# A third PSUM bank for one of five chains of products, and the work list of a fused convolution and SiLU layer written anew

## The chip, the cores and the metric

The kernel runs on one core of one Trainium2 chip. The metric is the device time of one launch in microseconds, as the median of several runs. All arithmetic is in fp32.

## The reference, cut to what matters

A causal depthwise convolution over time (seven taps, softmaxed per head), followed by a two-layer feed-forward block with SiLU:

```python
x: (8, 4096, 192)   weight: (8 heads, 7 taps)   w_in: (192, 2048)   w_out: (2048, 192)
w = softmax(weight, axis=-1)
conv[b, s, h, :] = sum_k w[h, k] * x_pad[b, s + k, h, :]      # six zeros ahead of each sequence
x1 = conv.reshape(32768, 192)
h  = x1 @ w_in                    # 32768 x 192 x 2048
g  = h / (1 + exp(-h))
out = g @ w_out                   # 32768 x 2048 x 192
```

## The kernel before, in words

**Tiling.** The 32768 tokens are cut into 32 blocks of 1024, and each block into two halves of 512. The 192 input channels are three pieces of 64, so a product of `h` contracts 64 rows: it uses half of TensorE's rows, and two products, one on partitions 0 to 63 ("row A") and one on 64 to 127 ("row B"), run side by side. The 2048 hidden channels are sixteen chunks of 128. Fifteen of these are worked in five groups of three, and one, the "plain" chunk, by itself.

**The products of h.** For a group, three chunks times two token halves are six outputs. Done directly they would need 18 products; the kernel does 15, from sums of weights (made once) and sums of inputs (`wins`, made for each block by VectorE). Token `P r.g` of the work list is product `r` of group `g` (line 623 in the profile). Eight or nine of the fifteen (`ON_B`) stand on row B. Products are added up in PSUM in three chains for a group, written in `CHAINS`: chain 0 is products 5, 2, 6, 1, 0, 14, in this order and all on row B (one exception: 14 of group 4); chain 1 is 3, 9, 7, 4, 8, all but 4 on row A; chain 2 is 12, 10 on row A. Products 13 and 11 go on top of sums that VectorE wrote to banks 5 and 6.

A chain's partial sums are read between its products. After product 5, 2, 6, 1 and 0 of chain 0 ScalarE copies the bank to a tile `u` (tokens `u5` to `u0`, line 672), after 14 it takes the SiLU (`S3`). Chains 1 and 2 are read by VectorE (tokens `X`, `a`, `b`, line 666), which adds or subtracts them to those `u`. So the next product of a chain, which writes to the same bank, waits for the engine that reads it. `S` tokens are the other SiLUs (line 684). The plain chunk is nine matmuls `L` (line 640), three of full width and three pairs of halves, in banks 7 and 3, evicted by the SiLUs `SL`.

**The output.** `g @ w_out` is done in tokens `D i.je` (line 739): each is four matmuls on four column groups of 32, which run side by side, over all 128 rows. There are 48 of them for a block, of one 512-wide slot each, except the eight with `i` = 5, which are 128 wide. Some read sums `t` that VectorE makes (line 707); the results are merged (`M`, `x`, `y`, `z`), turned (`o`) and stored (`st`). Output tile `osb` and the sums `t` share one pool of three buffers, in rotation.

An fp32 matmul stands in the trace as two passes, each with its weight load.

**The order.** Nothing is scheduled by the program: the order is a list, kept on every engine. `START` is the list for the first blocks, `PLAN` is run once for each later block, and each token issues its instructions in turn. A sign says whose work it is: none, the block itself; `-` one block back, `=` two back, `+` the next one. `ld` loads inputs, `i` turns them, `ha` sets the halo, `v` is one tap of the convolution, `sp` copies the result to both row groups (`dup`), `w` makes the input sums; all five are for the block after the one that their sign names. TensorE thus does, for each run of `PLAN`, one long row of 64-row products and one row of output products. In the list of before the output products are broken once: after twelve of them stand `-P8.3` and `P2.0`, then come the other 36.

**The banks.** PSUM has eight banks of 512 fp32 columns, all used. `chain_bank` gives chain `c` of group `g` its bank: the groups are taken in the order `QUEUE = (0, 4, 1, 2, 3)`, and

```python
    def chain_bank(g, c):
        return banks[(c * 2 + QUEUE.index(g) % 2) if c < 2 else 4]
    PLAIN_BANKS = (7, 7, 3)
    ACC = (7, 1, 3, 5, 6, 4, 0)      # banks of the output sums
```

so chain 0 has banks 0, 1, 0, 1, 0 for the five groups, chain 1 has 2, 3, 2, 3, 2, and chain 2 has 4.

Of the kernel before, what the change touches and what calls it, by code (L numbers as in the profile page):

```python
# [17 lines left out]
def kernel(  # L18
# [60 lines left out]


    PLAN = (
        "P5.0 v.20 -t.01 | -P10.3 -S3.2 | -P4.3 -S1.1 -S0.1 -sp.2 -a0.2 | -D1.31 u5.0 -t.03 "
        "-S4.3 | -D2.01 -S2.3 -t.02 | -D2.00 | -D0.00 -b5.3 | -D4.00 -a1.3 -S5.3 -t.10 -S5.4 "
        "| -D3.01 -S0.2 -S5.2 | -D5.00 -w.0 | -D1.00 v.00 -t.11 -S1.2 | -D0.31 | -D1.30 -w.1 "
        "| -D4.01 | -D2.10 -t.13 | -P8.3 | P2.0 v.11 | -D5.01 u4.0 v.01 | -D3.00 -S1.3 -t.12 "
        "| -D4.10 | -D4.11 -t.20 | -D2.11 | -D3.10 -t.22 | -D5.11 | -D0.10 -a0.3 | -D0.11 "
        "-t.21 -S0.3 | -D1.01 v.21 | -D2.20 -t.23 | -D0.30 v.22 | -D3.11 v.23 | -D2.21 v.02 "
        "| -D0.21 -w.2 | -D5.10 v.12 | -D0.20 -t.30 | -D0.01 | -D4.20 -y0.0 -t.31 -z1.0 | "
        "-D3.20 v.13 | -D4.21 -w.3 | -D3.21 -t.33 | -D2.31 -t.32 | -D1.10 | -D2.30 v.14 | "
        "-D1.20 v.24 -y2.0 -M1.0 | -D1.21 v.03 | -D1.11 | -D3.31 -y1.0 -M2.0 | -D3.30 v.25 | "  # L90
        "-D5.31 -M3.0 | -D5.21 | -D5.30 | -D4.30 -w.5 -M6.0 | -D5.20 | -D4.31 -x2.2 -x0.0 "
        "-M4.0 | P3.0 | P6.0 -x2.0 -x2.1 v.15 | L.01 | P5.4 u2.0 -M5.0 | L.00 | P1.0 X2.0 "
        "u5.4 v.26 | L.02 | P2.4 u0.0 v.04 | P0.0 | P9.0 SL.0 -w.4 -x1.0 | L.10 u1.0 X4.0 | "
        "L.12 u4.4 -o.1 | L.11 -x2.3 | P14.0 | P13.0 v.16 -st.1 SL.2 -o.3 | P11.0 | P7.0 "
        "S3.0 | P6.4 | P12.0 +ld.2 S4.0 a5.0 S2.0 | P5.1 | P3.4 b1.0 u2.4 | P4.0 | P10.0 "
        "X2.4 u5.1 +ld.0 | P2.1 | P9.4 a1.0 b5.0 | P1.4 | P8.0 u4.1 X4.4 SL.1 +ld.1 | P13.4 "
        "| P6.1 v.05 u0.4 a0.0 | P7.4 | P0.4 u2.1 v.06 S0.0 | P12.4 | P11.4 a5.4 u1.4 S2.4 | "
        "P3.1 | P1.1 -o.0 | P14.4 | P4.4 X2.1 u0.1 b1.4 | P0.1 | P9.1 S3.4 a1.4 S4.4 | P5.2 "
        "| P10.4 +i.2 u1.1 X4.1 | P14.1 | P8.4 u5.2 -M7.0 | P2.2 | P7.1 b5.4 S3.1 a0.4 | "
        "P13.1 | P5.3 u4.2 a5.1 | P12.1 | P6.2 +i.0 S2.1 sp.1 u5.3 | P3.2 | P4.1 b1.1 u2.2 "  # L100
        "S1.0 | P2.3 | P10.1 X2.2 S5.0 a1.1 | P1.2 | P13.2 u4.3 t.00 S0.4 | P6.3 | P8.1 S2.2 "
        "b5.1 u0.2 | P11.1 | P9.2 u2.3 a0.1 | P0.2 | P12.2 +i.1 S4.1 +ha.0 X4.2 | P1.3 | "
        "P3.3 u1.2 b1.2 | P11.2 | P7.2 u0.3 -st.3 X2.3 S1.4 | P10.2 | P0.3 a5.2 S4.2 | P9.3 "
        "-st.0 | P14.2 b5.2 u1.3 S5.1 -o.2 | P13.3 | P4.2 X4.3 -st.2 | P12.3 | P14.3 a1.2 | "
        "P7.3 | P11.3 b1.3 S3.3 sp.0 +v.10 | P8.2 a5.3"
    )
    START = (
        "=dp.31 =v.00 =v.10 =dp.45 =v.20 =dp.42 =dp.8 =dp.24 =dp.28 =dp.44 =dp.38 =dp.27 "
        "=dp.7 =dp.26 =dp.37 =dp.39 =dp.11 =dp.33 =dp.15 =dp.46 =dp.18 -ld.2 =dp.25 =dp.35 "
        "=dp.17 -ld.0 =dp.2 =dp.19 -ld.1 =dp.34 =v.21 =dp.41 =v.11 =dp.21 =v.22 =dp.16 =v.01 "  # L110
        "=v.23 =dp.40 =v.12 =dp.30 =v.24 =dp.23 =v.02 =v.25 =dp.20 =v.03 =dp.1 =v.26 =dp.13 "
        "=v.04 =sp.2 =dp.10 =v.13 =v.05 =dp.6 =v.14 =dp.22 =v.06 =dp.29 =v.15 =sp.0 =dp.4 "
        "=v.16 =go.1 =dp.12 -i.1 =sp.1 -i.2 =dp.47 -i.0 =dp.0 =dp.3 -ha.0 =dp.32 =dp.43 =w.0 "
        "=dp.36 -v.20 -v.00 =w.1 =dp.14 -v.10 -v.21 =dp.5 -v.01 -v.11 -L.01 -P5.0 =w.2 =dp.9 "
        "-u5.0 -v.12 -v.22 =cp.1 -P2.0 -L.00 =w.3 -P5.4 -L.02 -u4.0 -v.02 -P6.0 -P3.0 -SL.0 "
        "=cp.0 -L.10 -u2.0 -L.11 -u5.4 -X2.0 -L.12 =cp.2 -P1.0 -v.13 =w.5 -P2.4 -P12.0 -u0.0 "
        "=o.0 -P0.0 -P9.0 -u4.4 -SL.2 -P13.0 -P6.4 -u1.0 -X4.0 -v.23 -P14.0 -P3.4 -u2.4 -b1.0 "
        "-S2.0 -P7.0 -P1.4 -S3.0 =w.4 -X2.4 -P5.1 -P10.0 -u0.4 -a5.0 -P9.4 -P0.4 -u5.1 =o.1 "
        "-P13.4 -v.24 -P2.1 =st.1 -u1.4 -v.14 -P4.0 -P14.4 -u4.1 -b5.0 -S2.4 ld.1 -P11.0 "
        "-a1.0 -SL.1 -P12.4 -S3.4 =o.2 -P6.1 -S4.0 -P8.0 -X4.4 -P5.2 -u2.1 ld.0 -a0.0 -P7.4 "  # L120
        "-P11.4 -u5.2 -b1.4 -P1.1 -P3.1 -a5.4 -S4.4 =st.2 -P2.2 -P10.4 -u0.1 -X2.1 -P4.4 "
        "-P9.1 -u4.2 -b5.4 =st.0 -P0.1 -P12.1 -a1.4 -X4.1 -P6.2 ld.2 -P8.4 -u1.1 -v.03 -P14.1 "
        "-P7.1 -u2.2 -a0.4 -P11.1 -b1.1 -P13.1 -S3.1 -a5.1 -P5.3 -P3.2 -S2.1 -v.25 -S0.0 "
        "-P10.1 -P4.1 -X2.2 -u5.3 -S1.4 -P1.2 -P9.2 -a1.1 -S5.0 -v.04 -P2.3 -P8.1 -u0.2 -b5.1 "
        "-P0.2 -P13.2 -u4.3 -v.15 -S4.1 -P6.3 -a0.1 -P12.2 -u1.2 -X4.2 -P14.2 -P3.3 -u2.3 "
        "-b1.2 -S2.2 -P1.3 -P7.2 -v.05 -X2.3 -P10.2 -P11.2 -u0.3 -a5.2 -S0.1 -P9.3 -P0.3 "
        "-b5.2 -S4.2 -P4.2 -P12.3 -X4.3 -u1.3 -S3.2 -v.06 -P13.3 -P11.3 -S0.4 -v.16 -S1.0 "
        "-P14.3 -P7.3 -a1.2 -sp.1 -S2.3 -b1.3 -D1.01 -S3.3 -t.00 -S5.1 -D1.20 -S1.1 -a5.3 "
        "-S4.3 -sp.0 -D1.31 -t.02 -D0.31 -v.26 -P8.2 -P4.3 -t.01 -P10.3 P5.0 -D0.10 -b5.3 "
        "-sp.2 -t.03 -D0.01 -D1.11 i.1 i.2 -D5.00 -D3.01 -a0.2 i.0 -D3.00 -t.10 ha.0 -D5.01 "  # L130
        "-D2.01 -a1.3 +ld.0 -D2.00 -t.11 -D4.01 v.10 -w.0 -D4.00 -S5.2 +ld.1 -w.1 u5.0 -D2.10 "
        "-S5.4 v.11 -S5.3 -D1.30 -t.13 -S0.2 +ld.2 -S1.3 -P8.3 P2.0 -t.12 v.00 -S1.2 -D2.11 "
        "-a0.3 u4.0 v.20 -D0.00 -t.20 -S0.3 -D4.11 v.12 -D3.11 -t.21 -D4.10 -w.2 -D3.10 -t.23 "
        "-D5.10 -D1.10 v.21 -D0.21 -t.22 -D2.20 v.01 -D0.20 -w.3 v.22 -D5.11 -D4.21 -w.4 "
        "-D3.20 -t.30 -D0.30 v.13 -w.5 P6.0 P3.0 -t.31 -D1.00 v.14 -D4.20 -D5.20 -D2.21 "
        "-D3.21 -t.33 -D2.30 v.23 -D0.11 -t.32 -D1.21 -z1.0 v.15 u2.0 -D5.31 -D2.31 -y0.0 "
        "v.24 -D4.30 -M1.0 v.16 -D5.30 -D5.21 -D3.31 -M2.0 -x2.2 -x2.1 -D3.30 -y1.0 -y2.0 "
        "-D4.31 -x2.3 -M3.0 -x0.0 v.02 -x2.0 L.02 P1.0 v.25 L.01 P5.4 v.03 u0.0 L.00 X2.0 "
        "P0.0 u5.4 -M6.0 P2.4 P12.0 SL.0 -M4.0 u1.0 v.04 L.11 u4.4 L.12 -M5.0 P14.0 P13.0 "
        "b1.0 L.10 v.05 S3.0 P9.0 P6.4 -x1.0 -o.1 SL.2 P5.1 P10.0 u2.4 X4.0 S2.0 P3.4 P1.4 "  # L140
        "b5.0 u5.1 SL.1 P11.0 P7.0 X2.4 u0.4 v.06 P2.1 P9.4 S4.0 a5.0 P0.4 P13.4 u4.1 X4.4 "
        "P4.0 -M7.0 P12.4 S2.4 u1.4 P6.1 P7.4 a1.0 b1.4 P11.4 P8.0 u2.1 a5.4 P10.4 P1.1 S4.4 "
        "-o.3 S1.0 a0.0 P14.4 P4.4 u0.1 v.26 P3.1 P0.1 S3.4 b5.4 P5.2 X2.1 P12.1 u1.1 a1.4 "
        "P9.1 P14.1 u5.2 -o.2 P2.2 P13.1 b1.1 S3.1 X4.1 P8.4 P5.3 u4.2 +i.0 S2.1 P10.1 P6.2 "
        "+i.1 S5.0 sp.1 a0.4 P7.1 P11.1 u2.2 b5.1 S0.4 P3.2 P1.2 a5.1 u5.3 -st.2 S4.1 X2.2 "
        "P4.1 P12.2 S5.1 u0.2 P9.2 P2.3 a1.1 S0.0 P0.2 P8.1 u4.3 X4.2 +i.2 P6.3 P7.2 u1.2 "
        "a0.1 +ha.0 P11.2 P13.2 b1.2 u2.3 S1.4 a5.2 P3.3 P1.3 S2.2 -o.0 P10.2 P4.2 X2.3 u0.3 "
        "-st.0 S4.2 P0.3 P9.3 b5.2 t.00 -st.3 P14.2 P13.3 u1.3 P12.3 P14.3 X4.3 -st.1 a1.2 "
        "P7.3 P11.3 S3.3 b1.3 +v.10 P8.2 a5.3 sp.0"
    )  # L150
    QUEUE = (0, 4, 1, 2, 3)

    def pin(ins):
        return tc.keep_in_program_order(ins)
# [427 lines left out]
    sums, cmbs, accs, banks = {}, {}, {}, []  # L582
# [19 lines left out]
    XBANK = {2: 5, 4: 6}  # L602

    def chain_bank(g, c):
        return banks[(c * 2 + QUEUE.index(g) % 2) if c < 2 else 4]

    def columns(half):
        return slice(0, TB) if half is None else slice(half * TB // 2, (half + 1) * TB // 2)
# [1 line left out]
    def product(b, g, r, half=None):  # L610
        cols = columns(half)
        e = int(r in ON_B and (g, r) != SWAP)
        if r in RIGHT:
            rhs = rows(wins[b], e)[:, RIGHT[r], :]
        else:
            rhs = rows(dups[b], e)[:, SLOT[e][X_OF[r]], :]
        if r in (13, 11):
            to, first = banks[XBANK[2 if r == 13 else 4]], False
        else:
            c = next(c for c in range(3) if r in CHAINS[c])  # L620
            to, first = chain_bank(g, c), r == CHAINS[c][0]
        pin(
            nc.tensor.matmul(  # L623
                to[:, cols],
                raw(g, *LEFT[e][r], e),
                rhs[:, cols],
                start=first,
                stop=True,
                skip_group_check=True,
            )  # L630
        )
# [477 lines left out]
```

## Time and profile before

| what | value |
|---|---|
| median of 3 runs | 2371.1 us (2370.94 to 2371.49) |
| the profiled execution, time | 2371.36 us |
| the profiled execution, span | 2369.3 us |
| TensorE matmul busy | 2361.4 us (100%), 17630 instructions |
| VectorE busy | 2101.8 us (89%) |
| ScalarE busy | 1199.8 us (51%) |
| GpSimd busy | 95.4 us (4%) |
| granted TensorE clock | full in every slice |
| DMA | 106.56 MB, mean 45 GB/s |

The span is that of the profiled execution alone; 2.06 us of its time lie around the span. Matmuls overlap, two or four at a time, so the busy time of a group of matmuls is not a share of the span, and a busy TensorE may still stand still for a tenth of a microsecond between two matmuls: that is seen only in the distance between starts.

### The profile page before, as it was taken

To read this page: it belongs to the slowest core of one execution; us is meant where nothing else is said; L and a number is where in the kernel's file an instruction comes from. 1 tells how busy PE (TensorE), PEld (TensorE's weight loads), DVE (VectorE), ACT (ScalarE), POOL (GpSimd) and SP (SyncE) were. 2 spreads that over 40 slices of the span, in tenths; PEclk is the share of its full clock that TensorE was granted. 3 is DMA by queue.
4 is the path that set the end of the run, shared out by engine and by line. 5 is a ranking of instruction groups with operands and counts; after the bars stand their busy time and mean duration, and the time that the engine had idled before them with its cause. 6 is when DMAs were issued, how large, how long until landed. Compare 5 with 4: busy or idle time off the path is not lost.

```text
span 2369.3 us, 44036 instructions
## 1 busy us (share of the span) xinstructions
PE 2361.4 (100%) x17630; PEld 1061.7 (45%) x17630; DVE 2101.8 (89%) x2877; ACT 1199.8 (51%) x2275; POOL 95.4 (4%) x168
## 2 busy tenths in 40 slices
PE   9999999999999999999999999999999999999998
PEld 5344444444444444444444444444444444444443
DVE  8999898998988989888989889898889988898866
ACT  5345644456544465444564445654445644456443
POOL 4910000000000000000000000000000000000000
PEclk9999999999999999999999999999999999999999
DMA  7232212122211222122221212221122212222111
GB/s 157 57 59 39 52 29 48 29 52 52 42 37 31 49 52 52 26 40 39 52 53 33 43 29 52 52 48 31 33 47 52 52 27 41 39 52 52 23 27 18
DMA packets 451245, 106.56 MB, mean 45 GB/s; under 512 B 423584, under 2 KB 428704, under 8 KB 451040
## 3 DMA queue, kind: packets, MB, share of 16 engines
q1 hardware_dynamic: 447392, 101.78, 23.4%
q8 instruction: 138, 2.26, 0.4%
q0 software_dynamic: 448, 1.58, 0.3%
q10 hardware_dynamic: 3200, 0.39, 0.1%
q14 instruction: 67, 0.55, 0.1%
HBM read 31.46 MB, written 25.17 MB: 24 GB/s over the span
## 4 chain that ended last, share of the span: by engine, by line
PE 99%; DVE 0%; ACT 0%; issue 0%; ACTq 0%; DVEq 0%
PE ps L739 48%; PE ps L623 43%; PE ps L640 4%; PE ps L760 2%; PE ps L569 2%; PE ps L1008 1%; PE ps L421 0%; DVE cmb L161 0%; ACT u L161 0%; DVE g L666 0%; DVE t L707 0%; DVE osb L161 0%; DVE xt L463 0%; PE ps L447 0%; ACTq L942 0%
## 5 line engine op out<-in xcount | busy, mean ns | idle before, releaser
L623 PE MATMUL ps<-win,ws 64*128 64x512 f32 x1550 | 698.3, 609 | 0.0
L739 PE MATMUL ps<-g,wo 128*32 128x512 f32 x2976 | 681.2, 592 | 0.0
L623 PE MATMUL ps<-win,wr 64*128 64x512 f32 x1550 | 638.6, 598 | 0.0
L672 ACT COPY u<-ps 128x512 f32<-128x512 f32 x775 | 445.0, 587 | 281.7 <-PE ps L623 279.5
L739 PE MATMUL ps<-t,wo 128*32 128x128 f32 (+2 forms) x4528 | 523.8, 447 | 0.0
L739 PE MATMUL ps<-t,wx 128*32 128x512 f32 x2976 | 489.9, 592 | 0.6 <-DVE g L666 0.6
L497 DVE SCALAR_TENSOR_TENSOR nat<-xt,taps,nat 128x512 f32<-128x512 f32 x564 | 414.0, 754 | 2.3 <-ACT nat L494 1.1
L623 PE MATMUL ps<-dup,wr 64*128 64x512 f32 x868 | 410.0, 597 | 0.0
L684 ACT ACTIVATE g<-g 128x512 f32<-128x512 f32 x465 | 276.2, 628 | 177.4 <-DVE g L666 177.4
L707 DVE TENSOR_TENSOR t<-g,t 128x1024 f32<-128x1024 f32 x248 | 302.8, 1221 | 62.3 <-PE ps L739 61.2
L623 PE MATMUL ps<-dup,ws 64*128 64x512 f32 x682 | 339.9, 602 | 0.0
L707 DVE TENSOR_TENSOR t<-g 128x1024 f32<-128x1024 f32 x248 | 300.2, 1220 | 34.2 <-PE ps L739 30.6
L666 DVE TENSOR_TENSOR g<-u,ps 128x512 f32<-128x512 f32 x465 | 315.1, 682 | 15.2 <-PE ps L623 7.3
L623 PEld LDWEIGHTS ps<-win,wr 64*128 64x128 f32 x1550 | 238.7, 186 | 166.7 <-issue 94.7
L684 ACT ACTIVATE g<-ps 128x512 f32<-128x512 f32 x465 | 268.0, 598 | 88.1 <-PE ps L623 87.8
L623 PEld LDWEIGHTS ps<-win,ws 64*128 64x128 f32 x1550 | 244.5, 185 | 122.9 <-ACT u L672 61.9
L802 ACT COPY yx<-ps 32x512 f32<-32x512 f32 x150 | 87.0, 580 | 414.5 <-PE ps L739 412.9
L739 PEld LDWEIGHTS ps<-t,wo 128*32 128x32 f32 x4528 | 178.5, 110 | 243.5 <-issue 232.5
L666 DVE TENSOR_TENSOR ps<-u,ps 128x512 f32<-128x512 f32 x310 | 212.5, 685 | 42.1 <-PE ps L623 27.0
L739 PE MATMUL ps<-g,wx 128*32 128x512 f32 x1488 | 246.0, 594 | 0.0
L739 PEld LDWEIGHTS ps<-t,wx 128*32 128x32 f32 x2976 | 121.0, 110 | 260.5 <-issue 231.4
L739 PEld LDWEIGHTS ps<-g,wo 128*32 128x32 f32 x2976 | 169.3, 110 | 112.7 <-issue 112.4
(90 smaller groups left out, 1746.6 us busy)
## 6 DMA issues: line engine op xcount, KB each, us to landing
dup<-nat SPq DMA_DIRECT2D x345, 128.0 KB, 2.3
nat<-in_x_dram SPq DMA_DIRECT2D x382, 64.0 KB, 2.4
out_dram<-osb SPq DMA_DIRECT2D x376, 64.0 KB, 2.0
raw<-in_moe_w_out_dram SPq DMA_DIRECT2D x8, 384.0 KB, 3.6
raw<-in_moe_w_in_dram SPq DMA_DIRECT2D x12, 192.0 KB, 4.3
ws<-wr POOLq DMA_DIRECT2D x8, 192.0 KB, 5.1
raw<-in_moe_w_in_dram SPq DMA_DIRECT2D x6, 128.0 KB, 3.1
xt<-xt SPq DMA_DIRECT2D x31, 4.5 KB, 1.9
```

The costliest lines, as they stand in the source:

```text
L497: nc.vector.scalar_tensor_tensor(out=dst, in0=src, scalar=tap, in1=dst, op0=ALU.mult, op1=ALU.add)
L569: nc.tensor.matmul(hs[a, n, e], rows(wr[j], e)[:, a, k, :], rows(d, e)[:, n, k, :], start=k == 0, stop=k == NK - 1,)
L623: nc.tensor.matmul(to[:, cols], raw(g, *LEFT[e][r], e), rhs[:, cols], start=first, stop=True, skip_group_check=True,)
L640: nc.tensor.matmul(banks[PLAIN_BANKS[n and 1 + e]][:, cols], rows(wr[j] if own == e else ws[j], e)[:, a, k, :], rows(dups[b], e)[:, SLOT[e ...
L666: pin(nc.vector.tensor_tensor(out_, u, v, op=op))
L672: pin(nc.scalar.copy(us[b, g, o][:, cols], t1[:, cols]))
L684: pin(nc.scalar.activation(h, src, AF.Silu))
L707: pin(nc.vector.tensor_tensor(t[i // 2][:, i % 2, :], u, v, op=ALU.subtract))
L739: nc.tensor.matmul(accs[b][at][SQ * q : SQ * q + SQ, to], lhs[:, e, SQ * k : SQ * k + SQ], rhs[:, e, ts(q, TB // 4) if i == 5 else to], st ...
L760: nc.tensor.matmul(banks[DOWN_BANKS[k]][R * n : R * n + R, :], wo[j][:, a, e, R * k : R * k + R], gs[b, j, a][:, n, e, :], start=j == 0 an ...
L802: pin(nc.scalar.copy(to, acc[3 * (name[0] == "x") + k][n:P, :]))
L1008: nc.tensor.matmul(by_pe[k][n], rows(diag, n)[:, k, i, :], rows(xts[0], n)[:, k, i : i + TB], start=i == 0, stop=i == K - 1,)
```

## The change

Three things change. The function `chain_bank` reads its banks from a table, in which chain 0 of the third group of the queue (group 1) stands in bank 7, the bank of the plain chunk; all else is as before. The first product of a chain is marked as begun when it is issued. And both lists are written anew: every block has the same tokens as before, in another order, and the output products of a block stand in one row of 48 in `PLAN`.

```diff
     PLAN = (
-        "P5.0 v.20 -t.01 | -P10.3 -S3.2 | -P4.3 -S1.1 -S0.1 -sp.2 -a0.2 | -D1.31 u5.0 -t.03 "
...
-        "| -D4.01 | -D2.10 -t.13 | -P8.3 | P2.0 v.11 | -D5.01 u4.0 v.01 | -D3.00 -S1.3 -t.12 "
...
-        "-D5.31 -M3.0 | -D5.21 | -D5.30 | -D4.30 -w.5 -M6.0 | -D5.20 | -D4.31 -x2.2 -x0.0 "
-        "-M4.0 | P3.0 | P6.0 -x2.0 -x2.1 v.15 | L.01 | P5.4 u2.0 -M5.0 | L.00 | P1.0 X2.0 "
...
+        "P5.0 | -P8.3 -S3.2 -sp.2 v.00 -t.01 | -D1.31 -S2.3 -S5.2 | -D1.01 -a0.2 -S1.3 =st.2 "
+        "-a0.3 -S1.1 | -D1.11 -b5.3 -S0.2 | -D0.00 -S5.4 v.22 -sp.0 -S4.3 | -D2.01 -t.03 "
+        "-S5.1 -S1.2 | -D0.20 =st.0 -t.02 -S0.3 | -D1.21 -S5.3 v.01 | -D2.00 v.11 | -D5.01 "
+        "+ld.0 | -D0.30 v.02 | -D3.00 -t.10 | -D0.01 +ld.1 v.23 | -D0.31 v.24 | -D4.00 -t.11 "
+        "+ld.2 | -D3.01 -w.0 | -D4.01 | -D0.11 -t.13 | -D2.11 -w.1 | -D5.00 | -D4.11 -t.12 | "
...
+        "| P2.0 | L.00 -M4.0 -x2.1 -w.3 | L.01 | P5.4 u4.0 -w.4 | L.02 | P6.0 u5.4 v.15 | "
+        "P3.0 | P2.4 SL.0 v.16 u2.0 | L.12 -x2.3 X2.0 | L.11 -x2.2 u4.4 | L.10 -M5.0 | P9.0 "
...
+        "P4.3 S3.3 b1.3 | P8.2 a1.3 | P10.3 | P14.2 t.00"
     )
...
+    CHAIN_BANKS = ((0, 1, 7, 1, 0), (2, 3, 2, 3, 2), (4, 4, 4, 4, 4))
...
     def chain_bank(g, c):
-        return banks[(c * 2 + QUEUE.index(g) % 2) if c < 2 else 4]
+        return banks[CHAIN_BANKS[c][QUEUE.index(g)]]
...
             c = next(c for c in range(3) if r in CHAINS[c])
-            to, first = chain_bank(g, c), r == CHAINS[c][0]
+            to, first = chain_bank(g, c), r == CHAINS[c][0] and (b, g, c) not in begun
+            begun.add((b, g, c))
```

The bars in a list only group its tokens. The two rows of 64-row products from one row of output products to the next, in their order of issue (a star: of the block after; `L`: the plain chunk, whose last three on each row are half-width; `[D x12]`: twelve output products, which take both rows):

```
before, row B  P6.0 P5.4 P1.0 P2.4 P0.0 L L L P14.0 P11.0 P6.4 P5.1 P4.0 P2.1 P1.4 P6.1 P0.4 P11.4 P1.1 P4.4 P0.1
               P5.2 P14.1 P2.2 P5.3 P6.2 P4.1 P2.3 P1.2 P6.3 P11.1 P0.2 P1.3 P11.2 P0.3 P14.2 P4.2 P14.3 P11.3
               P5.0* P4.3 [D x12] P2.0* [D x36]
after, row B   P2.0 P5.4 P6.0 P2.4 L L L P1.0 P6.4 P5.1 P0.0 P11.0 P1.4 P4.0 P2.1 P0.4 P11.4 P6.1 P14.0 P4.4 P1.1
               P5.2 P0.1 P2.2 P5.3 P6.2 P11.1 P4.1 P2.3 P1.2 P6.3 P11.2 P0.2 P1.3 P4.2 P14.1 P0.3 P11.3 P14.3 P4.3
               P14.2 P5.0* [D x48]
before, row A  P3.0 L L L P9.0 L L L P13.0 P7.0 P12.0 P3.4 P10.0 P9.4 P8.0 P13.4 P7.4 P12.4 P3.1 P14.4 P9.1 P10.4
               P8.4 P7.1 P13.1 P12.1 P3.2 P10.1 P13.2 P8.1 P9.2 P12.2 P3.3 P7.2 P10.2 P9.3 P13.3 P12.3 P7.3 P8.2
               P10.3 [D x12] P8.3 [D x36]
after, row A   L L L P3.0 L L L P9.0 P13.0 P3.4 P7.0 P12.0 P9.4 P13.4 P10.0 P7.4 P8.0 P12.4 P14.4 P3.1 P10.4 P9.1
               P13.1 P8.4 P7.1 P12.1 P3.2 P10.1 P9.2 P8.1 P13.2 P7.2 P3.3 P12.2 P9.3 P10.2 P7.3 P12.3 P13.3 P8.2
               P10.3 P8.3 [D x48]
```

## The prediction

> **What bounds the kernel now.** First the page: the span, the engines, the granted clock, the chain that ended last.
>
> ```profile
> span 2369.3 us, 44036 instructions
> PE 2361.4 (100%) x17630; PEld 1061.7 (45%) x17630; DVE 2101.8 (89%) x2877; ACT 1199.8 (51%) x2275; POOL 95.4 (4%) x168
> PEclk9999999999999999999999999999999999999999
> PE 99%; DVE 0%; ACT 0%; issue 0%; ACTq 0%; DVEq 0%
> ```
>
> TensorE is busy all the way at full clock and is the whole chain. So a gain must come out of TensorE's own row: fewer matmuls (there are not fewer: both lists have the same tokens) or closer ones. The view by windows cuts one block into its stretches (columns: length; busy time of PE, PEld, DVE, ACT, POOL; clock; DMA share and GB/s): twelve output products, the inserted pair P8.3 and P2.0, 36 output products, the long row of products of h.
>
> ```profile
> 1014.79:1024.51 9.72, 9.72 (x96) 2.90 (x96) 8.23 (x10) 5.29 (x10) 0.00 (x0) 1.00 0.43 96
> 1024.51:1025.64 1.13, 1.13 (x12) 0.37 (x12) 1.13 (x3) 0.00 (x0) 0.00 (x0) 1.00 0.00 0
> 1025.64:1052.20 26.56, 26.56 (x291) 8.96 (x290) 22.95 (x29) 4.85 (x9) 0.00 (x0) 1.00 0.00 1
> 1052.20:1087.58 35.38, 35.38 (x168) 20.59 (x172) 33.01 (x51) 27.25 (x53) 0.11 (x1) 1.00 0.37 63
> ```
>
> One block takes 72.79 us (72.80 in nearly all blocks). Now the timeline of TensorE around the pair, and a stretch of the long row with its readers (start, length, engine, line).
>
> ```profile
> 1023.97 0.61 PE L739 MATMUL ps<-t,wx 128*32 128x512 f32 x3
> 1023.99 0.59 PE L739 MATMUL ps<-g,wo 128*32 128x512 f32 x1
> 1024.51 1.13 PE L623 MATMUL ps<-win,wr 64*128 64x512 f32 x4
> 1025.57 1.28 PE L739 MATMUL ps<-t,wo 128*32 128x128 f32 x16
> ```
>
> ```profile
> 1060.63 0.59 PE L623 MATMUL ps<-dup,wr 64*128 64x512 f32 x1
> ...
> 1060.87 0.69 DVE L666 TENSOR_TENSOR u<-u,ps 128x512 f32<-128x512 f32 x1 [0.17 <-PE ps L623]
> ...
> 1061.06 0.59 PE L623 MATMUL ps<-dup,wr 64*128 64x512 f32 x1
> ...
> 1061.07 1.01 PE L623 MATMUL ps<-win,ws 64*128 64x512 f32 x2
> ...
> 1061.61 0.69 PE L623 MATMUL ps<-dup,ws 64*128 64x512 f32 x1
> 1061.68 0.59 ACT L672 COPY u<-ps 128x512 f32<-128x512 f32 x1 [0.15 <-PE ps L623]
> ...
> 1062.15 0.59 PE L623 MATMUL ps<-dup,ws 64*128 64x512 f32 x1
> 1062.32 0.29 PEld L623 LDWEIGHTS ps<-win,wr 64*128 64x128 f32 x2 [0.42 <-ACT u L672]
> 1062.35 0.67 PE L623 MATMUL ps<-win,wr 64*128 64x512 f32 x1
> ...
> 1062.86 0.59 PE L623 MATMUL ps<-win,wr 64*128 64x512 f32 x1
> ```
>
> What to see is distance between starts. Two passes of one row follow each other after 0.4285 us when nothing waits (1060.63, 1061.06), so a product is a slot of 0.857 us. In the second piece P5.1 (row B) starts at 1060.63, its copy begins 0.62 after the start of its last pass, lasts 0.59, and P2.1, the next in the same bank, starts at 1062.35 and its second pass 0.51 later instead of 0.43: 0.08 lost. On row A P10.0 stands two slots behind P12.0 in bank 4; it starts 0.05 after VectorE's subtraction ended (1061.56), 0.12 late, and its second pass again 0.105 late. The 0.42 that the weight load "waited" is not the loss: loads run ahead.
>
> I added up, over blocks 5 to 28, what each start is later than 0.4285 per pass (0.1085 for 128 columns). Per block: output products 40 x 2 x 0.4285 + 8 x 2 x 0.1085 = 36.02; products of h 40.5 slots on each row x 0.857 = 34.71; together 70.73. Losses: row B 1.79, row A 1.59, each time that output products begin 0.116. **Row B, 70.73 + 1.79 + 2 x 0.116 = 72.75, is the 72.80.** So 2.0 us a block is all there is to gain, some 2.8%.
>
> **The loss rule.** From a product's first pass to a free bank for the next one: 0.4285 + 0.626 to the reader's start + the reader, and the next must start 0.158 (0.053 and the 0.105 of the late second pass) after the reader's end to lose nothing. With ScalarE's copy (0.587, row L672) 1.80 us, with VectorE's add (0.682, row L666) 1.89. Two slots are 1.714: a product two slots behind its forerunner in the bank loses 0.085 behind ScalarE (traced: 0.082 at P2.1, P6.1, P14.1, P6.3) and 0.18 behind VectorE when that comes at once (traced: 0.224 at P10.0, 0.149 at P9.1, 0.258 at P10.1; mean 0.21); three slots (2.57) lose nothing. If a stall already lies within the two slots, it has paid: of fifteen two-slot reuses of chain 0 in the old list ten lose. Stalls also pass to the other row through the queue: P9.0 (0.238) stands behind the waiting P0.0, P10.4 (0.117) behind P0.1: 0.355 for row A.
>
> **The change part by part.**
>
> *Output products in one run.* P8.3 and P2.0 go to the ends of the long row, with their slots. What goes is one entry and one return: 0.115 + 0.105 ahead of and within the pair, 0.091 + 0.025 after it, 0.336 a block. The Trainium skill (TensorEngine Tiling (Array Packing), Tiling Modes) says that a change of tiling mode drains TensorE; TensorE: Matmul & The Clock Gate (Step-by-step: what each phase is for) puts the drain at about 128 cycles, 53 ns at 2.4 GHz. By that, two drains would be 0.107 a block, 3.1 us over 29 blocks; by the row 9.7 us. I take the row.
>
> *The third bank and the order of chain 0.* With group 1 in bank 7, the chains 0 of three groups may be woven into each other. Counted on the lists, two-slot reuses on chain 0 fall from fifteen to seven: P6.0, P2.4, P0.1, P2.2, P6.2, P6.3, P14.3. P2.4 and P2.2 have a stall within their two slots; five lose 0.085. Row B: 0.22 (entry) + 0.43 = 0.65 instead of 1.79, before what row A passes to it. Bank 7 itself is free: the plain chunk's SiLU has 2.5 slots until P5.1, and the output sum there is read well before the next plain chunk.
>
> *Row A gains less and becomes the bound.* Its chains still have banks 2, 3 and 4, and the new order packs them tighter: two slots behind VectorE stand nine products (P9.1, P8.1, P9.2, P10.1, P10.2, P9.3, P7.3, P12.3, P8.3) where there were six. Five of the nine have another's stall within their two slots (P8.1 and P9.2 that of P10.1, P10.2 that of P9.3, P12.3 that of P7.3, P8.3 that of the closing products); P9.1, P10.1, P9.3, P7.3 pay 0.21 each, 0.84. The plain chunk's second part stands two slots behind its first, as before, but no longer behind P9.0's stall: 0.09. Passed over from row B: in proportion to the waits there 0.355 x 7/15 = 0.17, unreduced 0.36; I take 0.30, since A's queue is no emptier. With the entry 0.22: **row A 1.45.**
>
> The Trainium skill speaks against more here (TensorEngine Tiling (Array Packing), PSUM Bottleneck): tiling speeds up TensorE, not the emptying of PSUM, which may become the limit. VectorE is busy 33.01 of 35.38 us of the long row. If that were the limit, a bank would move nothing and only the mode change would count, -9.7 us; by my count of stalls the sum is -13.2. The difference is the part of row B's loss that lay above row A's.
>
> *Sum.* Per block before 1.79 + 0.232 = 2.02, after 1.45 + 0.116 = 1.57: -0.454; over the 29 blocks that `PLAN` runs in full -13.2 us.
>
> *What moves on the other engines.* VectorE and ScalarE do the same operations; about 31 us of VectorE's listed work falls on each of the two stretches, as before, so its adds come at once about as often. The loads' twelve issues (0.54 us apart on SP) move from the long row into the output row, some 30 us ahead of the turns that need them: hidden, and without that cover each us late would cost one. `START` is rewritten too; it has two fewer mode changes (-0.7), and its filling is not to be priced from this trace: I take nothing, +-2 us.
>
> **The rivals.**
>
> *No change:* row A's stalls grow to what row B had (1.79): then -0.116 a block, -3.4 us, 2367.7. Needs P9.1, P10.1, P9.3, P7.3 at 0.29 each; for it, VectorE's 89%; against, the highest traced is 0.258.
>
> *The bank moves nothing:* the third bank was no limit beside VectorE, only the joining of the runs pays: -9.7, 2361.4.
>
> *More:* row A loses only its four waits and the entry (1.15), nothing is passed over: -0.75 a block, -22, 2349.
>
> *Slower, through the stores:* the two-blocks-old stores `=st.2` and `=st.0` move into the output row, behind `sp` copies on the same queue. The output tile shares three buffers with the sums `t`, and `t.10` takes the buffer that `=st.0` reads. Between them lie five output products, 4.3 us; three issues 0.54 apart and the landing (median 2.0 us in the row of DMA issues) take 3.6. VectorE would stand at `t.10`, and behind it two taps and `t.11`: 3.6 us of work, with seven output products, 6.0 us, until D2.11 reads `t.11`. So 0.7 + 2.4 = 3.1 us of slack in all; from 5 us after issue on, each us beyond costs one us a block: at 6 us +29 - 13, 2387. Against it: stores land after 2.0 in every stretch of this trace where the loads run beside them.
>
> **The numbers.** The profiled execution took 2371.36, span 2369.3; the median is 0.26 lower. Span 2369.3 - 13.2 = 2356.1, time 2358.2, as a median 2358.0. About 0.2%, 4.7 us, is what a measurement of this kernel can tell from no change. Chances: forecast 0.68, more 0.08, bank moves nothing 0.10, all faster: 0.86; no change 0.08; slower 0.06. The likeliest case's own range, with row A between 1.25 and 1.65 and +-2 for the start, is 2351 to 2365; the bank that moves nothing lies within. With half of the case of more, 2350 to 2366.
>
> **What would show it.** In the profile after: one row of output products of about 36.3 us and one long row of about 36.1, block to block 72.35; no L623 piece between pieces of L739; the weight loads' waits for ACT u fewer than 249. Starts of chain 0 no longer 0.08 late at P2.1, P6.1, P14.1, P0.3; late at P9.1, P10.1, P9.3, P7.3 by 0.15 to 0.26. The count of stalls is wrong if row B is still the longer row, or if a block takes under 72.0 or over 72.65; the stores' rival is right if VectorE stands at L709 (the sums' line after) for a landing store.

## The result, and the profile after

The changed kernel takes 2359.27 us as a median (2358.95 to 2359.34), against 2371.03 for the kernel before (2370.94 to 2371.49) on the same chip: 11.8 us less, a ratio of 0.9950 with a 95% interval of 0.9933 to 0.9967. The forecast was 2358.0.

The page of the changed kernel: span, engines, and the shares of the chain that ended last.

```profile
span 2357.4 us, 43991 instructions
PE 2349.2 (100%) x17630; PEld 1043.8 (44%) x17630; DVE 2110.6 (90%) x2877; ACT 1179.4 (50%) x2275; POOL 105.7 (4%) x168
PE 99%; DVE 1%; ACT 0%; issue 0%; ACTq 0%; DVEq 0%
```

The same number of matmuls in 12 us less, and TensorE is still the whole chain. VectorE is no less busy than before: nothing was taken off it.

The view by windows of the changed kernel, one block (columns as in the prediction): the row of output products, and the long row of products of h.

```profile
1011.70:1047.92 36.22, 36.22 (x387) 12.09 (x386) 32.98 (x39) 9.50 (x19) 0.00 (x0) 1.00 0.30 52
1047.92:1084.08 36.16, 36.16 (x172) 20.04 (x176) 32.63 (x52) 27.36 (x54) 0.11 (x1) 1.00 0.18 34
```

Together 72.38 us a block, where it was 72.80. There is one row of output products, and it stands within 0.1 us of its floor: 36.02 of pure slots and 0.116 for its entry make 36.14 of its 36.22. What is left to lose lies in the long row. (Each row of TensorE has 40.5 slots of products of h in a block; of the fifteen products of a group eight stand on row B, of group 4 seven, where the text above has "eight or nine".)

The waits of the weight loads of the products of h (who waits, for whom: us in all, times, the longest), before and after.

```profile
PEld ps L623 <- ACT u L672: 113.9, 249, 0.8
PEld ps L623 <- DVE ps L666: 22.5, 66, 0.7
PEld ps L623 <- DVE g L666: 17.1, 69, 0.7
PEld ps L623 <- DVE u L666: 10.3, 31, 0.4
```

```profile
PEld ps L625 <- ACT u L674: 53.0, 154, 1.4
PEld ps L625 <- DVE ps L668: 42.5, 123, 0.8
PEld ps L625 <- DVE u L668: 32.9, 88, 0.6
PEld ps L625 <- DVE g L668: 30.5, 96, 0.8
```

Before there were 249 waits for ScalarE's copies, 113.9 us in all, and 166 for VectorE's three kinds of sums, 49.9 us. Now it is 154 and 53.0 against 307 and 105.9. The waits have changed engines: more of them are now for VectorE's reading of chains 1 and 2 than for ScalarE's reading of chain 0. A load's wait is not itself a loss; what each wait costs stands in the account below. One of them, P9.1 behind X2.1, in the timeline of the changed kernel:

```profile
1063.14 1.02 PE L625 MATMUL ps<-win,wr 64*128 64x512 f32 x4
...
1064.32 0.70 DVE L668 TENSOR_TENSOR ps<-u,ps 128x512 f32<-128x512 f32 x1 [0.59 <-PE ps L625]
...
1064.43 0.59 PE L625 MATMUL ps<-dup,ws 64*128 64x512 f32 x1
...
1065.07 0.69 PE L625 MATMUL ps<-win,ws 64*128 64x512 f32 x1
...
1065.60 0.83 PE L625 MATMUL ps<-win,ws 64*128 64x512 f32 x2
...
1066.23 0.69 DVE L668 TENSOR_TENSOR ps<-u,ps 128x512 f32<-128x512 f32 x1 [0.63 <-PE ps L625]
```

The first line is two passes each of P3.1 and of P4.4 beside it; P3.1's last pass starts at 1063.57. VectorE stood idle, so it was not another operation that kept P9.1 waiting; its read ended at 1065.02. P9.1 starts 0.05 later, where its slot had begun at 1064.86 (0.43 after 1064.43): 0.21 lost, and its second pass comes 0.53 instead of 0.43 after the first: another 0.105. This is a round trip through one bank, not a busy engine.

The hand-over to VectorE is part of that round trip, and it is not always the same. X2.1 begins 0.75 us after the start of P3.1's last pass (1064.32 less 1063.57); X4.1, the sum behind P9.1, begins 0.63 after that of P9.1 (1066.23 less 1065.60). By the semaphores in the trace, X4.1, X4.3 and b5.2 wait for TensorE alone, and each begins 0.63 after the last pass's start. X2.2, X2.3, b1.1 and b1.2 wait for ScalarE's copy as well, and each begins 0.70 after it; X2.1 is of this kind, and its copy had long ended, at 1063.08. Which part of the hand-over costs the difference was not tested, nor why X2.1 takes 0.05 more than the rest.

**The account of the long row.** Added up as in the prediction, over blocks 5 to 28, first and second pass together, in us a block:

| row A | late | row B | late |
|---|---|---|---|
| entry (L.00) | 0.225 | entry (P2.0) | 0.219 |
| L.12 | 0.155 | P6.0, P6.2, P6.3, P14.3 | 0.083 each |
| P9.1 | 0.315 | P0.1 | 0.119 |
| P10.1 | 0.256 | P2.4 | 0.052 |
| P9.3 | 0.264 | P4.3 | 0.137 |
| P7.3 | 0.196 | P14.2 | 0.411 |
| small ones | 0.06 | small ones | 0.08 |
| **sum** | **1.47** | **sum** | **1.35** |

Row A is the longer one, as forecast, by only 0.12. (Late: how much later its two passes start than their slots; for instance P9.1, 0.21 and 0.105.)

### The profile page after: what moved, and what is told of

Same layout as the page of the kernel before. It is cut to its first block, busy times and chain, and to the rows that moved or that the text cites. A ratio compares the mean times of both kernels' runs of the same rounds, so it can differ in the third digit from the quotient of the medians.

```text
span 2357.4 us, 43991 instructions
## 1 busy us (share of the span) xinstructions
PE 2349.2 (100%) x17630; PEld 1043.8 (44%) x17630; DVE 2110.6 (90%) x2877; ACT 1179.4 (50%) x2275; POOL 105.7 (4%) x168
## 4 chain that ended last, share of the span: by engine, by line
PE 99%; DVE 1%; ACT 0%; issue 0%; ACTq 0%; DVEq 0%
PE ps L741 47%; PE ps L625 45%; PE ps L642 2%; PE ps L762 2%; PE ps L570 2%; PE ps L1010 1%; PE ps L422 0%; DVE t L709 0%; DVE g L668 0%; DVE cmb L819 0%; DVE cmb L162 0%; ACT u L162 0%; ACT yx L804 0%; DVE osb L162 0%; DVE win L532 0%
## 5 line engine op out<-in xcount | busy, mean ns | idle before, releaser
L741 PE MATMUL ps<-g,wo 128*32 128x512 f32 x2976 | 691.9, 592 | 0.0
L625 PE MATMUL ps<-win,wr 64*128 64x512 f32 x1550 | 691.3, 595 | 0.0
L625 PE MATMUL ps<-win,ws 64*128 64x512 f32 x1550 | 674.3, 603 | 0.6 <-ACT u L674 0.6
L741 PE MATMUL ps<-t,wo 128*32 128x512 f32 (+2 forms) x4528 | 536.6, 446 | 0.5 <-DVE t L709 0.5
L625 PE MATMUL ps<-dup,wr 64*128 64x512 f32 x868 | 423.8, 590 | 0.0
L709 DVE TENSOR_TENSOR t<-g 128x1024 f32<-128x1024 f32 x248 | 299.9, 1220 | 61.1 <-PE ps L741 41.0
L709 DVE TENSOR_TENSOR t<-g,t 128x1024 f32<-128x1024 f32 x248 | 302.7, 1221 | 30.0 <-PE ps L741 24.7
L625 PEld LDWEIGHTS ps<-win,wr 64*128 64x128 f32 x1550 | 261.4, 186 | 148.3 <-issue 62.4
L668 DVE TENSOR_TENSOR g<-u,ps 128x512 f32<-128x512 f32 x465 | 305.7, 673 | 10.1 <-PE ps L625 1.4
L625 PE MATMUL ps<-dup,ws 64*128 64x512 f32 x682 | 280.9, 602 | 0.0
L686 ACT ACTIVATE g<-g 128x512 f32<-128x512 f32 x465 | 268.4, 633 | 15.3 <-DVE g L668 15.3
L807 ACT COPY cmb<-ps 96x512 f32<-96x512 f32 x30 | 17.5, 583 | 403.8 <-PE ps L741 403.8
```

Source lines behind the costliest of these rows:

```text
L625: nc.tensor.matmul(to[:, cols], raw(g, *LEFT[e][r], e), rhs[:, cols], start=first, stop=True, skip_group_check=True,)
L668: pin(nc.vector.tensor_tensor(out_, u, v, op=op))
L686: pin(nc.scalar.activation(h, src, AF.Silu))
L709: pin(nc.vector.tensor_tensor(t[i // 2][:, i % 2, :], u, v, op=ALU.subtract))
L741: nc.tensor.matmul(accs[b][at][SQ * q : SQ * q + SQ, to], lhs[:, e, SQ * k : SQ * k + SQ], rhs[:, e, ts(q, TB // 4) if i == 5 else to], st ...
```

## The experiments

Each is one edit of one of the two kernels. The next table sets the traced block beside 70.78 us (the 70.73 of the prediction and 0.05 that the count of pure slots had left out, read off the changed kernel) plus 0.116 for each run of output products plus the loss of the longer row.

| kernel | runs of output products | row A | row B | worked out | block traced | median |
|---|---|---|---|---|---|---|
| before | 2 | 1.59 | 1.79 | 72.80 | 72.80 | 2371.0 to 2371.4 |
| changed | 1 | 1.47 | 1.35 | 72.37 | 72.38 | 2359.27 |
| new_broken | 2 | 1.69 | 1.57 | 72.70 | 72.71 | 2368.87 |
| old_bank3 | 2 | 1.59 | 1.78 | 72.79 | 72.79 | 2372.29 |
| new_bank2 | 1 | 2.68 | 2.56 | 73.58 | 73.57 | 2396.18 (one) |
| b_relief | 1 | 1.47 | 0.94 | 72.37 | 72.37 | 2359.15 |
| a_wait | 1 | 1.73 | 1.61 | 72.63 | 72.63 | 2366.76 |
| a_free | 1 | 1.40 | 1.28 | 72.30 | 72.31 | 2357.49 |
| a_free_all | 1 | 1.00 | 0.81 | 71.90 | 71.89 | 2346.57 |

The agreement of the two columns of blocks is for the most part bookkeeping: slots and late starts come from the same trace as the block, and along one row they add up to it. What the table tests is that the step from the longer row to the output products stays at 0.116 in all nine kernels. That the longer row sets the time is tested by b_relief and a_wait.

new_broken, old_bank3, new_bank2 and late_store (which is not in the table) ran beside the kernel before at 2371.39 us, the last four of the table at 2371.19, the changed kernel at 2371.03.

**new_broken: the changed kernel, its output products broken once more.**

```diff
-"P5.0 | -P8.3 -S3.2 -sp.2 v.00 -t.01 | -D1.31 -S2.3 -S5.2 | -D1.01 -a0.2 -S1.3 =st.2 -a0.3 ..."
+"-S3.2 -sp.2 v.00 -t.01 | -D0.00 | -D0.01 -S2.3 -S5.2 | P5.0 | -P8.3 | -D1.31 | -D1.01 -a0.2 -S1.3 =st.2 -a0.3 ..."
```

D0.00 and D0.01 leave their later places; nothing else moves.

> The new list and the three banks, but in PLAN the pair P5.0 and -P8.3 stands behind the first two output products instead of ahead of them, so that the row of output products is broken once again in every block (the two output products ahead of it are D0.00 and D0.01, so that none of them waits for the SiLU of P14.2 in bank 1). My account: one entry and one return of the tiling mode more, 0.336 us a block over 29 blocks, +9.7: about 2369.0 us, block to block 72.71, and no stall of the long row changed. By a drain of 53 ns each way: +3.1, 2362.4, block to block 72.49. If the break itself is free: 2359.3.

Measured 2368.87 (2368.57 to 2369.47); ratio to before 0.9990 (0.9983 to 0.9996). The chain of its trace, one block:

```profile
1014.95 1.85 PE ps L741 x16
...
1017.86 34.50 PE ps L741 x368
...
1087.66 1.85 PE ps L741 x16
```

72.71 us from one entry to the next, 0.33 more than the changed kernel. The products at the break are late by the amounts that the pair of before showed: P8.3 0.120 and 0.105, P5.0 0.114 and 0.105, then 0.116 for the second entry of output products; all other stalls of the long row stay where they were. One entry and return costs 0.33 us a block and 9.6 us between the two medians (9.2 if each is set against the kernel before that ran beside it). The 3.1 us that the prediction weighed, an estimate from the drain of about 128 cycles, 53 ns, in the Trainium skill (TensorE: Matmul & The Clock Gate, Step-by-step: what each phase is for), would be a third of it.

**old_bank3: the kernel before with the third bank alone.**

```diff
+    CHAIN_BANKS = ((0, 1, 7, 1, 0), (2, 3, 2, 3, 2), (4, 4, 4, 4, 4))
-        return banks[(c * 2 + QUEUE.index(g) % 2) if c < 2 else 4]
+        return banks[CHAIN_BANKS[c][QUEUE.index(g)]]
```

In both lists `SL.1`, a read of bank 7, moves up beside `SL.2`, so that the bank is free in time.

> The old lists with the new table of banks: chain 0 of group 1 in bank 7 (the plain chunk's SL.1 is moved up beside SL.2 in both lists, so that bank 7 is free for it). My account: the two-slot waits of the old list lie within one group's chain, where a third bank does nothing; only P5.3 behind P14.1 (0.09) and the like go, so 0 to -0.1 us a block: 2368 to 2371 us, P2.1, P6.1, P0.1, P14.1 still late. If the bank by itself is what pays: row B falls to row A's 1.59, -0.2 a block, 2365 us or less.

Measured 2372.29 (2371.86 to 2372.86), 1.3 us above the range that was expected; ratio 1.0004 (0.9996 to 1.0013): no gain. The stall of P5.3 behind P14.1 is gone, but P6.2, which it had covered, is now 0.082 late; P2.1, P6.1, P0.1 and P14.1 are late as before, because in the old list the chains of the groups are not woven into each other there. Row B loses 1.78, as it did. A bank that the order of issue does not use is worth nothing here.

**new_bank2: the new list with two banks.**

```diff
-    CHAIN_BANKS = ((0, 1, 7, 1, 0), (2, 3, 2, 3, 2), (4, 4, 4, 4, 4))
+    CHAIN_BANKS = ((0, 1, 0, 1, 0), (2, 3, 2, 3, 2), (4, 4, 4, 4, 4))
```

> The new list with the old banks: chain 0 of groups 0, 1 and 3 all in bank 0. Group 1's chain begins in the new list before group 0's has ended, so the two are added up in one bank, which changes that part of the sums; the number and order of instructions is as in the new list. My account: the new list needs the bank, reuses of one and two slots come up again at P5.1, P1.1, P0.1, P14.3: +0.5 to +1.5 us a block, 2374 to 2403 us. If the bank moves nothing and the order alone pays: within 2 us of 2359.3.

One run, 2396.18 us, so without an interval; a block of 73.57: 1.19 more than with three banks, in nearly all blocks of the trace. P0.1 is now 0.71 late, P13.1 behind it in the queue 0.65, P14.3 0.57, P9.1 0.52. So list and bank need each other: the list without the bank is worse than the kernel before, the bank without the list does nothing.

**late_store: the output tile's store just ahead of the sums that want a buffer.** In the changed kernel `=st.0` moves behind D3.00, directly ahead of `-t.10`.

```diff
-"| -D0.20 =st.0 -t.02 -S0.3 | ... | -D3.00 -t.10 | ..."
+"| -D0.20 -t.02 -S0.3 | ... | -D3.00 =st.0 -t.10 | ..."
```

> The new list, but the stores =st.0 stand directly ahead of t.10, five output products (4.3 us) later. My working of the stores' rival: 0.7 + 2.4 = 3.1 us of slack, so 1.2 us a block are lost at D2.11, +35, about 2394 us, and VectorE stands at line 709 for a landing store of 64 KB in every block. If VectorE has no slack of its own behind t.10: 3.6 to 4 us a block, 2465 to 2475 us. If three buffers are enough all the same: 2359.3.

One run, 2486.57 us: some 4.5 us a block, where 1.2 had been expected. The waits and the timeline of VectorE say that it is not the wait that had been priced:

```profile
DVE t L709 <- PE ps L741: 201.0, 74, 6.0
PE ps L741 <- DVE t L709: 85.2, 28, 3.5
DVE t L709 <- DMA out_dram<-osb: 3.5, 1, 3.5
```

```profile
1069.07 2.08 DVE L498 SCALAR_TENSOR_TENSOR nat<-xt,taps,nat 128x512 f32<-128x512 f32 x3
1076.76 1.23 DVE L709 TENSOR_TENSOR t<-g 128x1024 f32<-128x1024 f32 x1 [5.61 <-PE ps L741]
```

VectorE stands 5.61 us ahead of `t.10`, and a TensorE read ends it, not a store; TensorE then waits for the sums, once a block (28 times). The read that ends it is the second pass of D4.01, which began at 1076.03: with the store later the three buffers go round in another order, and `t.10` gets the buffer of the sums `t.00` and `t.01`, which D4.00 and D4.01 still have to read. And `=st.0` now comes behind the loads `ld.0` on SP.

A part of the 4.5 is not a wait at all. After TensorE has stood still, its granted clock falls to half for 3.41 us in 16 of the blocks; the first line is a whole block in which it does not, the second such a fall in the next block (the clock is the third number from the end):

```profile
1218.29:1294.64 76.35, 73.22 (x553) 36.60 (x552) 65.56 (x90) 36.88 (x72) 0.63 (x1) 1.00 0.23 41
1312.55:1315.94 3.39, 3.39 (x35) 1.83 (x28) 3.39 (x4) 0.00 (x0) 0.00 (x0) 0.50 0.00 0
```

A block without it takes 76.35 us in most cases, 3.97 more than in the changed kernel; with it 77.3 to 78.2; the mean is 76.88. Why it comes only in some blocks, no run here shows.

Two things changed beside the one meant, so this run does not measure the rival of the stores. It shows that a store's place in the list bears on which buffer comes next, and that VectorE then stood 5.61 us for a read of TensorE.

**b_relief: row B alone made shorter.** P14.2's 0.41 is the largest loss of row B: it stands in the queue behind P10.3 of row A, whose weight load waits for VectorE. Its place is exchanged with that product's.

```diff
-"P4.3 S3.3 b1.3 | P8.2 a1.3 | P10.3 | P14.2 t.00"
+"P4.3 S3.3 b1.3 | P8.2 a1.3 | P14.2 | P10.3 t.00"
```

> The changed kernel with its last two products of h in the other order of issue: P14.2 (row B) ahead of P10.3 (row A). In the changed kernel P14.2 starts 0.41 us late, behind the waiting P10.3, the largest single loss of row B. Theory (row A sets the end of the long row: losses of 1.47 on A and 1.35 on B): P14.2's loss goes from row B, the block stays at 72.38 us within 0.03, time 2359.3. Rival 1 (the longer row is B, or the close of the row counts whole): -0.41 us a block, 71.97, time 2347. Rival 2 (losses of both rows count by half, since stalls pass to and fro in the one queue): -0.2 a block, 2353.

Measured 2359.15 (2358.88 to 2359.6); ratio 0.9949 (0.9934 to 0.9963): the time of the changed kernel. The end of the long row in the timeline, first the changed kernel, then b_relief:

```profile
1083.36 0.59 PE L625 MATMUL ps<-dup,wr 64*128 64x512 f32 x1
1083.49 0.59 PE L625 MATMUL ps<-win,wr 64*128 64x512 f32 x1
1084.01 0.63 PE L741 MATMUL ps<-g,wx 128*32 128x512 f32 x3
```

```profile
1083.46 0.59 PE L625 MATMUL ps<-dup,wr 64*128 64x512 f32 x1
1083.56 1.02 PE L625 MATMUL ps<-win,wr 64*128 64x512 f32 x2
1084.51 0.63 PE L741 MATMUL ps<-g,wx 128*32 128x512 f32 x3
```

The `dup` product is P5.0, the last of row B; the `win` product is P8.3, the last of row A. From the last pass of P5.0 to the first output product it is 0.65 us in the changed kernel and 1.05 in b_relief: row B is done 0.40 earlier and then waits. From the last pass of P8.3 it is 0.52 in both (in b_relief the second of the pair, 0.43 after 1083.56). Row A sets the end.

**a_wait: one more wait on row A.**

```diff
-"| P13.4 | P4.0 u0.4 X4.4 -w.5 | P10.0 | P2.1 a1.0 ..."
+"| P10.0 | P4.0 u0.4 X4.4 -w.5 | P13.4 | P2.1 a1.0 ..."
```

> The changed kernel with P10.0 and P13.4 (row A) exchanged: P10.0 then stands two slots behind P12.0 in bank 4 instead of three, with VectorE's subtraction between them, and no other stall lies in these two slots. Theory (row A is the bound, a two-slot reuse behind VectorE loses about 0.21 to 0.25): a new stall of that size at P10.0, passed on to P4.0 of row B, the block 72.38 + 0.23 = 72.6, 28 blocks, time 2365.7 (2364.5 to 2367). Rival (VectorE's pace sets the row, a wait at one place is made up at the next): no change, 2359.3.

Measured 2366.76 (2366.49 to 2367.32), 7.5 more than the changed kernel, at the upper end of what was expected; ratio 0.9981 (0.9973 to 0.9990). Two rows of output products in the chain of its trace, 72.63 apart:

```profile
1014.56 36.22 PE ps L741 x384
...
1087.19 36.22 PE ps L741 x384
```

P10.0 is 0.258 late and the block goes from 72.38 to 72.63: the whole of it arrives at the end, though some 26 us of the long row follow it. P4.0 on row B, behind it in the queue, is late by the same 0.258.

**a_free: one wait of row A taken away.** VectorE does as many operations as before, but one of them reads no bank.

```diff
-            add(banks[XBANK[o]], used(b, g, o), t2)
+            u = used(b, g, o)
+            add(banks[XBANK[o]], u, u if (g, o) == (1, 2) else t2)
```

> The changed kernel, in which VectorE's addition X2.1 takes its tile u twice and does not read the bank of P3.1 (this part of the sums is changed, the work of every engine stays). P9.1, the most delayed product of row A (0.315 us in all), then waits for nobody. Theory (absorption: a stall in the queue pays for later ones): P9.1's loss of about 0.3 goes, but row B's losses at P0.1 and P6.2, which it had covered, now pass to row A (0.08 each): -0.1 us a block (-0.05 to -0.15), 72.28, time 2356.5. Rival 1 (stalls add): row A falls to 1.16 and row B to 1.35 minus its share, at least -0.25 a block, 2352. Rival 2 (VectorE's pace): no change, 2359.3.

Measured 2357.49 (2357.23 to 2357.96); ratio 0.9942 (0.9927 to 0.9956). P9.1's 0.315 is gone, and the block is shorter by 0.07 only: P13.1 is now 0.131 late, behind the waiting P0.1 of row B, P12.1 0.082 behind P6.2, and P10.1 0.293 instead of 0.256. The stall at P9.1 had covered the first two; the 0.04 at P10.1 was not traced to a cause.

**a_free_all: the four waits of row A taken away.** The same for X2, X4, b1 and b5 of groups 1, 2 and 3.

```diff
+            add(banks[XBANK[o]], u, u if g in (1, 2, 3) else t2)
...
-            add(c, c, t3, ALU.subtract)
+            add(c, c, c if (g, o) in ((1, 1), (1, 5), (2, 1), (2, 5), (3, 1), (3, 5)) else t3, ALU.subtract)
```

> The changed kernel, in which VectorE's X2 and X4 additions and b1 and b5 subtractions of groups 1, 2 and 3 take a tile of their own twice instead of a bank (this part of the sums is changed; VectorE does as many operations of the same size as before). The four VectorE waits of row A, P9.1, P10.1, P9.3 and P7.3 (1.03 us together), go. Theory (round trips of single banks set row A, with absorption): what they had covered comes up: P8.1 and P8.3 (two slots behind VectorE, 0.2 each) and row B's P0.1 and P6.2 (0.08 each): 1.03 - 0.55 = -0.5 us a block, 71.9, time 2345 (2342 to 2349). Rival 1 (VectorE's throughput: busy for nine tenths of the span, it sets the pace wherever it has to be waited for): the waits move to other products, under -0.1 a block, 2357 or more. Rival 2 (stalls add): -1.03 a block, 2330.

Measured 2346.57 (2346.23 to 2346.91), 12.7 less than the changed kernel; ratio 0.9895 (0.9881 to 0.9910). The engines in its page, two rows of operations of its trace (VectorE's sums that read no bank and that read one; both write to a bank), and two rows of output products in its chain, 71.89 apart:

```profile
PE 2335.5 (100%) x17630; PEld 979.9 (42%) x17630; DVE 2101.4 (90%) x2877; ACT 1178.8 (50%) x2275; POOL 109.7 (5%) x168
L668 DVE TENSOR_TENSOR ps<-u 128x512 f32<-128x512 f32 x186 | 128.6, 692 | 12.3 <-ACT u L674 12.2
L668 DVE TENSOR_TENSOR ps<-u,ps 128x512 f32<-128x512 f32 x124 | 85.1, 686 | 12.7 <-PE ps L625 6.9 <-ACT u L674 4.2 <-ACT g L687 1.5
```

```profile
1007.50 36.22 PE ps L742 x384
...
1079.39 36.22 PE ps L742 x384
```

VectorE does the same 2877 operations, they take as long (692 ns against 686), and it is busy for the same nine tenths of the span; yet the block falls by 0.49. Row A now loses 1.00: its entry and L.12 as before, and P13.1 0.131, P12.1 0.082, P8.1 0.181, P8.3 0.162, each of which a longer wait had covered. Of 1.03 us taken away 0.56 came back in this way.

## Why the prediction was right, point by point

- **Row B bound the old kernel, row A the new one.** Held. In the changed kernel b_relief and a_wait show the two sides of it: 0.41 off row B is worth nothing, 0.26 on row A is paid whole. That row B bound the old kernel is read from its account alone (1.79 against 1.59); no run shortened one row of the old list by itself.
- **The joined runs, -0.336.** Held: new_broken gives 0.33 back. Here the row of the trace was right and the estimate from a drain was not.
- **Chain 0 needs the third bank and the order together.** The prediction never priced them apart except in a rival; old_bank3 and new_bank2 show that the bank alone gives 0 and its absence from the new list costs 1.19 a block. "The bank moves nothing" was nearer than its chance of 0.10 said: the joining is 9.2 to 9.6 of the 11.8 us, and the list and the bank without it, new_broken against the kernel before, bring 2.5 us (ratio 0.9990, 0.9983 to 0.9996). Small, but there, and so that rival falls. By the accounts row B gave up more (1.79 to 1.57), and row A, at 1.69, took over the bound after the first 0.1 of it.
- **The loss rule and its absorption.** Held in kind: 0.082 to 0.083 at P6.0, P6.2, P6.3 and P14.3, nothing at P2.2. P2.4, counted as fully covered, lost 0.05, and P9.1 lies beyond the 0.15 to 0.26 that was named for row A's waits. a_free and a_free_all show absorption at work: stalls come up that a longer one had covered.
- **Row A 1.45.** Traced 1.47, but by errors that cancel. The four waits cost 1.03, not 0.84 (four times 0.21), and most of the difference is a misreading of the old trace. P9.1 did not lose 0.149 there and P10.4 0.117; P9.1 lost 0.264 and P10.4 nothing:

```profile
1068.07 0.70 DVE L666 TENSOR_TENSOR ps<-u,ps 128x512 f32<-128x512 f32 x1 [0.48 <-PE ps L623]
...
1068.23 0.59 PE L623 MATMUL ps<-dup,ws 64*128 64x512 f32 x1
...
1068.68 1.26 PE L623 MATMUL ps<-win,ws 64*128 64x512 f32 x4
...
1069.78 0.59 PE L623 MATMUL ps<-dup,ws 64*128 64x512 f32 x1
```

The line of four is two passes each of P0.1 and of P9.1, which bear the same names. Row A's slot for P9.1 begins at 1068.66, 0.43 after the pass at 1068.23; X2.1 has read its bank at 1068.77, and P9.1 starts at 1068.82. The last of the four passes begins at 1069.35 (the line's end less 0.59), and P10.4 follows 0.43 after it, on time. With 0.224, 0.264 and 0.258 the mean is 0.25, and four waits make 0.99. The four differ by the hand-over: P7.3, behind a sum that waits for TensorE alone, loses 0.196, the other three 0.256 to 0.315. The plain chunk lost 0.155 instead of 0.09. What row B passes over was set at 0.30, from a 0.355 that held P10.4's 0.117, and is about 0.06, because row A's own waits covered it; a_free_all brought 0.21 of it back (P13.1 and P12.1).
- **Row B 0.65 before what A passes to it.** Traced 1.35. With P14.2's pass-over gone (b_relief) it is 0.94. The difference to 0.65 is P4.3 (0.137, behind VectorE, not counted), P0.1 (0.119 instead of 0.085), P2.4 and small ones. It did not matter, since row A was longer, but the margin was 0.12 and not 0.8 less pass-over, as the sum suggested.
- **The sum.** -0.454 a block over 29 blocks was -13.2; traced, -0.42 over 28 blocks that repeat in full, -11.8, the start about +0.4 and the end about -0.5 on top: -11.9 in the span. The start, taken at 0 +-2, was small.
- **The stores.** The rival's place was right, its price was not met. Its slack of 3.1 us is worked out 0.65 too high: of the five output products between the store and `t.10` one, D5.01, is 128 wide, so they take 3.65 us and not 4.3. In the changed kernel VectorE does stand at L709 for landing stores (its rows of waits):

```profile
DVE t L709 <- PE ps L741: 65.7, 83, 2.4
DVE t L709 <- DMA out_dram<-osb: 11.0, 12, 3.4
```

Twelve waits, 11.0 us on VectorE in all, and the block does not show them. Eleven, of at most 1.24 us, lie in blocks of 72.37 to 72.38, as all others are; the longest, 3.4, lies in the row of output products at 2242.07 us, the last of its length, where VectorE has less to do (busy for 23.07 us, against 32.98 in the row before); this row takes 36.22 like the rest. The mark that the prediction named for this rival (VectorE standing at L709) was too weak a mark; it should have been VectorE standing there *and* TensorE waiting for the sums in every block, as it does in late_store. What a landing costs that comes later than these was not measured.

## What to carry to other kernels

Where two rows of a tiled TensorE share a queue, count the late starts of each row by itself: in this kernel only the longer row was worth work. Such a count splits up the time of a traced block; what the next list will take has to be forecast stall by stall, and here that came out right by errors that cancelled. Where two products of one form run side by side, tell their records apart by what each waits for before you price them. A stall taken away seldom pays in full, because it had paid for others behind it; list what stands two slots behind the same bank, and what stands behind the other row's waits, before you price it. A VectorE that is busy for 90% need not be the limit: here the round trips of single banks cost 12.7 us, which came back when the reads were left out and VectorE's work was not.

## What the runs showed of the hardware that was not expected

- A product that starts late loses twice: it starts about 0.05 us after the reader's end (P9.1: 1065.07 after 1065.02), and its second pass comes 0.105 us late, also where it only stood in the queue behind a waiting product of the other row (P4.0 in a_wait: 0.153 and 0.105).
- VectorE's sum of 128x512 fp32 into a bank takes 692 ns when it reads SBUF alone and 686 ns when it reads a bank too (a_free_all).
- In late_store TensorE stands still for some 3 us in every block (3.13 us ahead of 1080.62), and in 16 of its blocks the granted clock then is 0.50 for 3.41 us. In the changed kernel, whose TensorE never stands that long within the blocks, it is full there.
- One break in a row of output products costs 0.33 us a block at full clock, three times the estimate of 0.107 that the prediction draws from the drain; which part of it is the change of tiling and which the weight loads, which there start only with their products (1084.01 us for those of the first output products of a row), was not separated.
